# Loads of turned queries moved from SyncE's to ScalarE's DMA queue, and the last projections of a linear-attention and gated-FFN kernel put in a fixed order

## The chip, the cores and the metric

The kernel runs on one core of a Trainium2 chip. The metric is the device time of one launch in microseconds (us), the median of several runs. A core has five engines that run side by side and wait for each other through semaphores: TensorE (PE, matrix products; PEld is its weight load), VectorE (DVE), ScalarE (ACT), GpSimd (POOL) and SyncE (SP), which here only issues DMAs. Each engine executes its own list of instructions strictly in the order of the program: an instruction that waits holds up everything behind it on its engine, DMA issues included.

## The reference

Linear attention with two softmaxes, then a gated feed-forward product. Shapes: q, k, v are 8 batches x 8 heads x 576 positions x 64; x is 4608 tokens x 512; w_a and w_b are 512 x 1536; w_out is 1536 x 512.

```
q_s = exp(q - max(q, -1));  q_s = q_s / (sum(q_s, -1) + 1e-9)     # over the head's 64
k_s = exp(k - max(k, 2));   k_s = k_s / (sum(k_s, 2) + 1e-9)      # over positions
kv  = einsum('bhsd,bhse->bhde', k_s, v)
x   = einsum('bhsd,bhde->bhse', q_s, kv)  -> [B*S, H*D]
out = ((x @ w_a) * (x @ w_b)) @ w_out
```

## The kernel before

The 4608 tokens are cut into 9 chunks (c = 0 to 8) of T = 512. All weights stay on the chip or in scratch memory as pairs of a rounded value and a remainder (`split`, L76: a cast on ACT, a subtraction on DVE), so that each product is three matmuls. While PE works on chunk c, the attention of chunk c + 1 is made in between, in small pieces that the class `Spread` hands out (`attend`).

**The feed-forward part of a chunk.** A loop over i = 0 to 5 (L665) takes two of the twelve 128-wide blocks of w_a and w_b at a time. The products with w_a and w_b are made by a scheme with seven block products instead of eight (`product`, L443, 12 matmuls of 256 columns each, into the PSUM tiles kx, ky, ka, kp), with additions on DVE (u, cc) between them. The weights of each block product, `ws`, come from scratch memory with one DMA of 512 KB each (`get_w`, L165) into eight buffers. The gate's two results per i are split into gh and gl (`g_split`, L437). Their product with w_out (`project`, L463: 4 token blocks t times 3 matmuls of 512 columns, into four PSUM tiles po) is put off: it goes on the list `pend`, and `run_pending` takes it up while the next i is under way. For the last i of the last chunk the two `run_pending` calls in the loop are left out (`if not end`), and all that is pending, the blocks f = 8, 9, 10 and 11, is run after the loop (L724).

**The end of a chunk.** After f = 11 `store` (L473) copies the four po tiles to SBUF (ot) and issues one DMA of 256 KB for each (L481). In chunks 0 to 7 ACT copies the whole row; in the last chunk ACT copies the left half of each row and then DVE the right half.

**The attention of chunks 2 to 8.** The queries are loaded twice. The first load (`q_load`) has tokens on partitions; `q_stats` takes maxima and sums from it, and `q_stats_out` (L330) turns these with a matmul (pst) and writes them to scratch memory (dq, L338). The second load has the queries turned, features on partitions (`q_turned`): per pair of heads g a tile qtt (256 KB, L344) and the maxima and reciprocals of the sums, broadcast over 64 partitions by two DMAs of 256 KB (mr, L347). `q_exp` (L354 on DVE, L355 on ACT) makes the exponentials, splits them into qh and ql, `x_product` (L381) multiplies them with the context into px, and L559 on DVE scales px by the second half of mr into xf. qtt shares two buffers with the keys' tiles (kt), and mr has two buffers: the DMAs for the third g wait until the first g's are done with.

**What sets the order.** Program order is not source order. The kernel is built with `schedule_with_timeline_sim=True`: a scheduler places every instruction on its engine's list by its own estimate of times. `tc.issue_after(ins)` tells it to place what follows not before the instruction named.

Of the kernel before, what the change touches and what calls it, by code (L numbers as in the profile page):

```python
# [23 lines left out]
A11, S2, S3, S1, A12, S4, A22 = range(7)  # L24
B11, T2, T3, T1, B21, B22, T4 = range(7)
# [4 lines left out]
def linear_attention_then_gated_ffn(  # L30
# [18 lines left out]
    nc = tc.nc  # L49
    B, NP, P, J, _, D = k.shape  # L50
# [3 lines left out]
    NF = 2 * NI  # L54
    T = 512
    H = T // 2
    TT = T // P
    NCH = NT // T
    LATE = NCH - qt_late.shape[0]
# [25 lines left out]
    wo = {}  # L85
# [255 lines left out]
    def q_turned(c, g, dq):  # L341

        qt = sb.tile([P, T], F32, name="qtt", tag="kt")
        nc.sync.dma_start(out=qt, in_=qt_late[c - LATE, g])  # L344
        mr = sb.tile([P, 2, T], F32, name="mr", bufs=2)
        for h in range(2):
            nc.sync.dma_start(  # L347
                out=mr[h * D:(h + 1) * D].rearrange("d w t -> d (w t)"),
                in_=dq[g, h].unsqueeze(0).broadcast_to([D, 2 * T]),
            )  # L350
        return qt, mr
# [91 lines left out]
    def product(pt, w, x, first):  # L443

        for n in range(2):
            i = 0
            for c in range(2):
                for wp, xp in ((0, 0), (0, 1), (1, 0)):
                    nc.tensor.matmul(  # L449
                        pt[:, n], w[:, n, wp, c], x[:, xp, c],  # L450
                        start=(first and n == 0 and i == 0), stop=(i == 5),
                        skip_group_check=True,
                    )
                    i += 1

    def project_first(f, g, po):
        for t in range(TT):
            nc.tensor.matmul(
                po[t], g[:, t * P:(t + 1) * P], wo[f][:, 1].bitcast(F32),
                start=(f == 0), stop=(f == NF - 1),  # L460
            )

    def project(f, ghl, po):  # L463
        gh, gl = ghl
        for t in range(TT):
            ts = slice(t * P, (t + 1) * P)
            for i, (a, w) in enumerate(((gh, 0), (gh, 1), (gl, 0))):
                nc.tensor.matmul(  # L468
                    po[t], a[:, ts], wo[f][:, w],
                    start=(f == 0 and i == 0), stop=(f == NF - 1 and i == 2),  # L470
                )

    def store(c, po):  # L473
        for t in range(TT):
            ot = sb.tile([P, DM], F32, name="ot", tag="wr", bufs=4)
            if c == NCH - 1:
                nc.scalar.copy(out=ot[:, 0:H], in_=po[t][:, 0:H])
                nc.vector.tensor_copy(out=ot[:, H:], in_=po[t][:, H:])
            else:
                nc.scalar.copy(out=ot, in_=po[t])  # L480
            nc.sync.dma_start(out=out[c * T + t * P:c * T + (t + 1) * P, :], in_=ot)  # L481
# [168 lines left out]
    def run_pending(last_only=False):  # L650

        if not pend:
            return
        f, ghl, c, po = pend.pop(0)
        (project if c else project_first)(f, ghl, po)
        if f == NF - 1:
            store(c, po)

    last = None
    for c in range(1, NCH):  # L660
        more = c + 1 < NCH
        attend = Spread(attention_tasks(c + 1) if more else [], 3 * NI - 3 - (1 if c == 1 else 0))
        po = None
        x, xo = xo, {}
        for i in range(NI):  # L665
            def operand(op):
                if c > 1:
                    return get_w(i, op)
                if op in (A11, A12, A22):
                    return get_w(i, op)  # L670
                w = split_w(sy[i][op])
                put_w(i, op, w)
                return w

            if more and i == NI - 1:
                x_operands(xfs[c + 1], early, xo)
            kx = ps.tile([P, 2, H], F32, name="kx", tag="k0")
            ky = ps.tile([P, 2, H], F32, name="ky", tag="k1")
            ka = ps.tile([P, 2, H], F32, name="ka", tag="k2")
            cc = sb.tile([P, 4, 2, H], F32, name="cc", bufs=1)  # L680
            u2 = sb.tile([P, 2, H], F32, name="u2", bufs=1)
            u3 = sb.tile([P, 2, H], F32, name="u3", bufs=1)
            if c > 1 or i > 0:
                attend(last)
            if c == 1:
                if i + 1 < NI:
                    sy[i + 1] = sums(i + 1)
                split_wo(2 * i)
                split_wo(2 * i + 1)
            product(kx, operand(A11), x[B11], True)  # L690
            product(ky, operand(S2), x[T2], True)
            nc.scalar.copy(out=u2, in_=kx)
            nc.vector.tensor_tensor(out=u2, in0=ky, in1=u2, op=ALU.add)  # L693
            product(ka, operand(S3), x[T3], True)
            last = nc.vector.tensor_tensor(out=u3, in0=ka, in1=u2, op=ALU.add)
            if more and i == NI - 1:
                x_operands(xfs[c + 1], late, xo)
            end = c == NCH - 1 and i == NI - 1
            if not end:
                run_pending()  # L700
            attend(last)
            kp = ps.tile([P, 2, H], F32, name="kp", tag="k1")
            product(kp, operand(S1), x[T1], True)
            product(kx, operand(A12), x[B21], False)

            nc.vector.tensor_tensor(out=cc[:, 3], in0=kp, in1=u3, op=ALU.add)  # L706
            nc.scalar.copy(out=cc[:, 0, 0], in_=kx[:, 0])  # L707
            nc.vector.tensor_tensor(out=cc[:, 0, 0], in0=kx[:, 1], in1=cc[:, 0, 0], op=ALU.mult)
            last = nc.vector.tensor_tensor(out=cc[:, 3, 0], in0=cc[:, 3, 0], in1=cc[:, 3, 1], op=ALU.mult)
            if not end:  # L710
                run_pending()
            if po is None:
                po = [ps.tile([P, DM], F32, name=f"po{t}") for t in range(TT)]
            attend(last)
            product(kp, operand(S4), x[B22], False)
            nc.vector.tensor_tensor(out=cc[:, 1], in0=kp, in1=u2, op=ALU.add)  # L716
            nc.vector.tensor_tensor(out=cc[:, 1, 0], in0=cc[:, 1, 0], in1=cc[:, 1, 1], op=ALU.mult)  # L717
            g1 = g_split(2 * i, cc[:, 0:2, 0])
            product(ka, operand(A22), x[T4], False)
            nc.vector.tensor_tensor(out=cc[:, 2], in0=ka, in1=u2, op=ALU.add)  # L720
            last = nc.vector.tensor_tensor(out=cc[:, 2, 0], in0=cc[:, 2, 0], in1=cc[:, 2, 1], op=ALU.mult)
            g2 = g_split(2 * i + 1, cc[:, 2:4, 0])
            pend += [(2 * i, g1, c, po), (2 * i + 1, g2, c, po)]
    while pend:  # L724
        run_pending()


# [48 lines left out]
```

## Time and profile before

| | before |
|---|---|
| median of 3 runs (lowest, highest) | 991.0 us (990.97, 994.56) |
| the profiled execution's own time | 986.57 us |
| its span, first to last instruction | 984.5 us |
| DVE, ACT, POOL busy | 632.5, 391.7, 112.8 us |
| mean granted TensorE clock | 0.990 |
| DMA queue q1 (all loads and stores) | 282.57 MB, 81.9% of 16 engines' span |

Busy time is the time in which an engine executes; waiting and the issuing of DMAs are not in it. Idle time before a group of instructions is put down to what ended it. In the rows of the trace an instruction stands as line, engine, operation, tile written <- tiles read, with its number and then busy time and mean duration; SPq is the part of SyncE that waits and issues.

### The profile page before, as it was taken

The numbers are of one execution on the slowest core, as the hardware profiler recorded it, in microseconds if no ns is written. First come the engines' busy times: TensorE is split into PE (matmuls) and PEld (weight loads), VectorE is DVE, ScalarE is ACT, GpSimd is POOL, SyncE is SP. The second block draws the span as 40 slices with busy tenths as digits, with TensorE's granted clock in tenths as the row PEclk, the third lists the DMA queues.
The fourth block names the chain that finished last, engine by engine and source line by source line (L and its number), as shares of the span: only waits on it lengthen the run. The fifth ranks groups of instructions, "written<-read, shape, count | busy, mean of one in ns | idle before, by whom it ended". The sixth has DMA issues, their size and how long they took to land.

```text
span 984.5 us, 16997 instructions
## 1 busy us (share of the span) xinstructions
PE 948.7 (96%) x6171; PEld 854.0 (87%) x6171; DVE 632.5 (64%) x1259; ACT 391.7 (40%) x1087; POOL 112.8 (11%) x96
## 2 busy tenths in 40 slices
PE   3889999999999999999999999999999999999998
PEld 3757666899999999999999999999999999899996
DVE  7797786988686665656566657565656545653443
ACT  8666675542372325322442335223532263221111
POOL 3245344531000000000000000000000000000000
PEclk9799999999999999999999999999999999999999
DMA  9699858999989967997699779977998679767761
GB/s 346 228 412 397 340 207 293 358 332 303 307 279 338 321 241 280 334 334 259 240 339 328 267 258 341 320 264 252 337 295 295 232 282 288 269 230 262 256 212 46
DMA packets 93682, 283.64 MB, mean 288 GB/s; under 512 B 10848, under 2 KB 11424, under 8 KB 93600
## 3 DMA queue, kind: packets, MB, share of 16 engines
q1 hardware_dynamic: 93600, 282.57, 81.9%
q8 instruction: 49, 0.80, 0.3%
q14 instruction: 33, 0.27, 0.1%
HBM read 241.40 MB, written 37.98 MB: 284 GB/s over the span
## 4 chain that ended last, share of the span: by engine, by line
PE 70%; DMA 6%; DVE 2%; ACT 1%; issue 1%; SPq 0%; DVEq 0%
PE po L468 24%; PE kp L449 12%; PE ka L449 12%; PE kx L449 12%; PE ky L449 6%; DMA mr<-dq 4%; DMA qtt<-in_q_late 2%; PE pk L251 2%; PE px L381 2%; DMA dq<-sst 1%; DVE ws L82 0%; ACT qt L323 0%; SPq L347 0%; DVE ql L82 0%; ACT gh L79 0%
## 5 line engine op out<-in xcount | busy, mean ns | idle before, releaser
L468 PE MATMUL po<-wo_w,gh 128*128 128x512 f32 x768 | 226.5, 394 | 1.0 <-ACT gh L79 1.0
L449 PE MATMUL kx<-xo,ws 128*128 128x256 f32 x1152 | 164.8, 284 | 0.0
L449 PE MATMUL ka<-xo,ws 128*128 128x256 f32 x1152 | 163.1, 285 | 0.9 <-DVE cc L720 0.7
L468 PEld LDWEIGHTS po<-wo_w,gh 128*128 128x128 f32 x768 | 138.8, 189 | 27.3 <-ACT gh L79 1.4
L449 PE MATMUL kp<-xo,ws 128*128 128x256 f32 x1152 | 158.3, 284 | 1.1 <-DVE u L693 1.0
L449 PEld LDWEIGHTS ka<-xo,ws 128*128 128x128 f32 x1152 | 152.1, 192 | 4.5 <-DVE cc L720 0.9
L449 PEld LDWEIGHTS kx<-xo,ws 128*128 128x128 f32 x1152 | 151.9, 191 | 3.5 <-issue 0.5
L449 PEld LDWEIGHTS kp<-xo,ws 128*128 128x128 f32 x1152 | 148.2, 191 | 3.9 <-DVE u L693 1.2
L468 PE MATMUL po<-wo_w,gl 128*128 128x512 f32 x384 | 136.9, 395 | 0.0
L79 ACT CAST gh<-cc 128x512 fp32r<-128x512 f32 x96 | 57.6, 620 | 147.4 <-DVE cc L717 144.1
L716 DVE TENSOR_TENSOR cc<-kp,u 128x512 f32<-128x512 f32 x48 | 33.0, 688 | 89.1 <-PE kp L449 88.8
L323 ACT ACTIVATE qt<-qt,st 128x64 f32<-128x64 f32 x224 | 75.0, 336 | 34.7 <-DVE st L320 30.5
L468 PEld LDWEIGHTS po<-wo_w,gl 128*128 128x128 f32 x384 | 71.2, 188 | 15.3
L449 PE MATMUL ky<-xo,ws 128*128 128x256 f32 x576 | 78.5, 285 | 2.5 <-ACT xo L79 2.1
L426 PE MATMUL pt<-xo,ws 128*128 128x512 f32 x288 | 76.1, 415 | 3.0 <-ACT ga L433 3.0
L449 PEld LDWEIGHTS ky<-xo,ws 128*128 128x128 f32 x576 | 72.9, 192 | 3.2 <-ACT xo L79 2.4
L82 DVE TENSOR_TENSOR gl<-cc,gh 128x512 fp32r<-128x512 f32 x96 | 66.9, 704 | 9.6 <-ACT gh L79 9.4
L426 PEld LDWEIGHTS pt<-xo,ws 128*128 128x128 f32 x288 | 55.0, 194 | 19.3 <-ACT ga L433 4.0
L707 ACT COPY cc<-kx 128x256 f32<-128x256 f32 x48 | 17.7, 370 | 130.8 <-PE kx L449 122.1
L706 DVE TENSOR_TENSOR cc<-kp,u 128x512 f32<-128x512 f32 x48 | 32.9, 685 | 54.8 <-PE kp L449 54.8
L219 POOL PARTITION_ALL_REDUCE mx<-m x20 | 14.1, 704 | 467.2 <-DVE m L205 435.4
L355 ACT ACTIVATE qtt<-qtt 128x512 f32<-128x512 f32 x28 | 17.7, 633 | 103.9 <-DVE qtt L354 77.4
(127 smaller groups left out, 1241.8 us busy)
## 6 DMA issues: line engine op xcount, KB each, us to landing
ws<-dw SPq DMA_DIRECT2D x312, 512.0 KB, 5.2
dw<-ws SPq DMA_DIRECT2D x42, 512.0 KB, 5.0
mr<-dq SPq DMA_DIRECT2D x56, 256.0 KB, 6.5
raw<-in_w_ab SPq DMA_DIRECT2D x24, 512.0 KB, 7.9
out<-ot SPq DMA_DIRECT2D x36, 256.0 KB, 4.8
vt<-in_v SPq DMA_DIRECT2D x28, 325.0 KB, 7.3
qt<-in_q SPq DMA_DIRECT2D x32, 256.0 KB, 5.2
kt<-in_k SPq DMA_DIRECT2D x24, 320.0 KB, 5.8
```

Of the source, the lines that this page charges most:

```text
L79: nc.scalar.copy(out=hi, in_=src)
L82: nc.vector.tensor_tensor(out=lo, in0=src, in1=hi.bitcast(F32), op=ALU.subtract)
L251: nc.tensor.matmul(pk, kt[:, j].rearrange("p h d -> p (h d)"), vt[:, j], start=(j == 0), stop=(j == J - 1),)
L323: nc.scalar.activation(out=qt[:, j, h], in_=qt[:, j, h], func=AF.Exp, bias=st[:, h, 0, j:j + 1], accum_out=st[:, h, 1, j:j + 1],)
L355: nc.scalar.activation(out=qt, in_=qt, func=AF.Exp)
L381: nc.tensor.matmul(px[:, s], w, m[:, s], start=(i == 0), stop=(i == 2))
L426: nc.tensor.matmul(pt, w[:, wp], x[g][:, xp], start=(i == 0), stop=(i == 3 * NP - 1))
L449: nc.tensor.matmul(pt[:, n], w[:, n, wp, c], x[:, xp, c], start=(first and n == 0 and i == 0), stop=(i == 5), skip_group_check=True,)
L468: nc.tensor.matmul(po[t], a[:, ts], wo[f][:, w], start=(f == 0 and i == 0), stop=(f == NF - 1 and i == 2),)
L706: nc.vector.tensor_tensor(out=cc[:, 3], in0=kp, in1=u3, op=ALU.add)
L707: nc.scalar.copy(out=cc[:, 0, 0], in_=kx[:, 0])
L716: nc.vector.tensor_tensor(out=cc[:, 1], in0=kp, in1=u2, op=ALU.add)
```

## The change

Three edits. The two loads of `q_turned` are issued by ACT (`nc.scalar.dma_start`), which gives them ACT's DMA queue in place of SyncE's. Everything pending at the end goes behind the last block product (`ka` with A22) and, in f = 10 and 11, the token blocks are kept in turn (three matmuls of one t, then the next t). In the last chunk's `store`, rows are copied whole, t = 0 and 2 by DVE, t = 1 and 3 by ACT.

```diff
     def q_turned(c, g, dq):
 
         qt = sb.tile([P, T], F32, name="qtt", tag="kt")
-        nc.sync.dma_start(out=qt, in_=qt_late[c - LATE, g])
+        nc.scalar.dma_start(out=qt, in_=qt_late[c - LATE, g])
         mr = sb.tile([P, 2, T], F32, name="mr", bufs=2)
         for h in range(2):
-            nc.sync.dma_start(
+            nc.scalar.dma_start(
                 out=mr[h * D:(h + 1) * D].rearrange("d w t -> d (w t)"),
                 in_=dq[g, h].unsqueeze(0).broadcast_to([D, 2 * T]),
             )
...
-    def project(f, ghl, po):
+    def project(f, ghl, po, one_by_one=False):
         gh, gl = ghl
-        for t in range(TT):
-            ts = slice(t * P, (t + 1) * P)
-            for i, (a, w) in enumerate(((gh, 0), (gh, 1), (gl, 0))):
-                nc.tensor.matmul(
-                    po[t], a[:, ts], wo[f][:, w],
-                    start=(f == 0 and i == 0), stop=(f == NF - 1 and i == 2),
-                )
+        with ExitStack() as in_turn:
+            for t in range(TT):
+                ts = slice(t * P, (t + 1) * P)
+                for i, (a, w) in enumerate(((gh, 0), (gh, 1), (gl, 0))):
+                    ins = nc.tensor.matmul(
+                        po[t], a[:, ts], wo[f][:, w],
+                        start=(f == 0 and i == 0), stop=(f == NF - 1 and i == 2),
+                    )
+                if one_by_one:
+                    in_turn.enter_context(tc.issue_after(ins.ins))
 
     def store(c, po):
         for t in range(TT):
             ot = sb.tile([P, DM], F32, name="ot", tag="wr", bufs=4)
-            if c == NCH - 1:
-                nc.scalar.copy(out=ot[:, 0:H], in_=po[t][:, 0:H])
-                nc.vector.tensor_copy(out=ot[:, H:], in_=po[t][:, H:])
+            if c == NCH - 1 and t % 2 == 0:
+                nc.vector.tensor_copy(out=ot, in_=po[t])
             else:
                 nc.scalar.copy(out=ot, in_=po[t])
...
-        (project if c else project_first)(f, ghl, po)
+        if c:
+            project(f, ghl, po, c == NCH - 1 and f >= NF - 2)
+        else:
+            project_first(f, ghl, po)
...
-            product(ka, operand(A22), x[T4], False)
+            last_product = product(ka, operand(A22), x[T4], False)
...
-    while pend:
-        run_pending()
+    with tc.issue_after(last_product.ins):
+        while pend:
+            run_pending()
```

The scheduler moves instructions on all engines but POOL, whose list stays the same, from chunk 1's attention tasks on. Three places matter below.

The first is SyncE's list behind the store of the maxima of chunk 5 (dq_5569), while PE is in chunk 4. Before, the loads of mr and qtt stand between those of the weights (ws):

```order
L338 DMA dq_5569<-sst 64x128
L165 DMA ws<-dw_681 128x1024
L165 DMA ws<-dw_774 128x1024
L347 DMA mr<-dq_5569 64x1024
L344 DMA qtt<-in_q_late 128x512
L347 DMA mr<-dq_5569 64x1024 x3
L165 DMA ws<-dw_2305 128x1024
L165 DMA ws<-dw_2324 128x1024
L165 DMA ws<-dw_2374 128x1024
L195 DMA vt<-in_v 128x650
L344 DMA qtt<-in_q_late 128x512
```

and now SyncE's list goes on with the weights and the values vt alone:

```order
L338 DMA dq_5569<-sst 64x128
L165 DMA ws<-dw_681 128x1024
L165 DMA ws<-dw_774 128x1024
L195 DMA vt<-in_v 128x650
L165 DMA ws<-dw_2305 128x1024
L165 DMA ws<-dw_2324 128x1024
L165 DMA ws<-dw_2374 128x1024
L195 DMA vt<-in_v 128x650
```

All eight mr loads and four qtt loads of the chunk have left the list.

The second place is ACT's list a little later in the same chunk, from the second exponential (L355) to the casts of the gate (gh_5854 and gh_5874 are f = 2 and 3's, which PE's projections read). Before:

```order
L355 ACTIVATE qtt<-qtt 128x512
L79 CAST qh<-qtt 128x512
L79 CAST gh_5854<-cc 128x512
L692 COPY u_5882<-kx 128x512
L79 CAST gh_5874<-cc 128x512
```

and now:

```order
L355 ACTIVATE qtt<-qtt 128x512
L79 CAST qh<-qtt 128x512
L347 DMA mr<-dq_5569 64x1024 x2
L79 CAST gh_5854<-cc 128x512
L344 DMA qtt<-in_q_late 128x512
L79 CAST gh_5874<-cc 128x512
L698 COPY u_5882<-kx 128x512
L347 DMA mr<-dq_5569 64x1024 x2
```

Two loads stand ahead of the first cast and one ahead of the second; the first two wait for L559 to have read the mr tile whose buffer they refill, and the qtt load for DVE's ql.

The third place is the end of PE's list: the last matmuls of f = 9 (gh_10559), the last block product (kp with S4), and the beginning of f = 10 (gh_10663). The four po tiles are 9927 to 9930. Before:

```order
L468 MATMUL po_9927<-wo_w,gh_10559 128x512 x2
L468 MATMUL po_9927<-wo_w,gl_10560 128x512
L468 MATMUL po_9928<-wo_w,gh_10559 128x512 x2
L468 MATMUL po_9928<-wo_w,gl_10560 128x512
L449 MATMUL kp<-xo,ws 128x256 x12
L468 MATMUL po_9929<-wo_w,gh_10559 128x512 x2
L468 MATMUL po_9929<-wo_w,gl_10560 128x512
L468 MATMUL po_9930<-wo_w,gh_10559 128x512 x2
L468 MATMUL po_9930<-wo_w,gl_10560 128x512
L468 MATMUL po_9927<-wo_w,gh_10663 128x512 x2
L468 MATMUL po_9928<-wo_w,gh_10663 128x512 x2
```

and now:

```order
L470 MATMUL po_9927<-wo_w,gh_10559 128x512 x2
L470 MATMUL po_9927<-wo_w,gl_10560 128x512
L449 MATMUL kp<-xo,ws 128x256 x12
L470 MATMUL po_9928<-wo_w,gh_10559 128x512 x2
L470 MATMUL po_9928<-wo_w,gl_10560 128x512
L470 MATMUL po_9929<-wo_w,gh_10559 128x512 x2
L470 MATMUL po_9929<-wo_w,gl_10560 128x512
L470 MATMUL po_9930<-wo_w,gh_10559 128x512 x2
L470 MATMUL po_9930<-wo_w,gl_10560 128x512
L470 MATMUL po_9927<-wo_w,gh_10663 128x512 x2
L470 MATMUL po_9927<-wo_w,gl_10664 128x512
```

Nine matmuls stand between the last block product and f = 10, where there were six. On ACT, the cast of f = 10's gate (gh_10663) now stands ahead of that of f = 11's (gh_10683); before it stood behind it.

More of the change, by code (lines that the diff above doesn't have):

```diff
@@ L454, in product @@
                     i += 1
+        return ins
     def project_first(f, g, po):
@@ L461, in project_first @@
             )
-    def project(f, ghl, po):
+    def project(f, ghl, po, one_by_one=False):
         gh, gl = ghl
-        for t in range(TT):
-            ts = slice(t * P, (t + 1) * P)
-            for i, (a, w) in enumerate(((gh, 0), (gh, 1), (gl, 0))):
-                nc.tensor.matmul(
-                    po[t], a[:, ts], wo[f][:, w],
-                    start=(f == 0 and i == 0), stop=(f == NF - 1 and i == 2),
-                )
+        with ExitStack() as in_turn:
+            for t in range(TT):
+                ts = slice(t * P, (t + 1) * P)
+                for i, (a, w) in enumerate(((gh, 0), (gh, 1), (gl, 0))):
+                    ins = nc.tensor.matmul(
+                        po[t], a[:, ts], wo[f][:, w],
[3 more added lines that the diff above has]
+                    in_turn.enter_context(tc.issue_after(ins.ins))
     def store(c, po):
```

## The prediction

> **What bounds the kernel now.** I read the page's head first, then the busy time by stage, then what PE waited for, and last the chain of waits at the end.
>
> ```profile
> span 984.5 us, 16997 instructions
> PE 948.7 (96%) x6171; PEld 854.0 (87%) x6171; DVE 632.5 (64%) x1259; ACT 391.7 (40%) x1087; POOL 112.8 (11%) x96
> core 0: us, PE busy (x) PEld busy (x) DVE busy (x) ACT busy (x) POOL busy (x), PEclk, DMA share, GB/s
> 0.00:218.00 218.00, 190.16 (x904) 146.39 (x905) 174.30 (x308) 137.91 (x355) 92.35 (x72) 0.95 0.86 324
> 218.00:960.00 742.00, 738.97 (x5155) 690.83 (x5155) 449.02 (x936) 249.95 (x724) 20.44 (x24) 1.00 0.84 286
> 960.00:984.50 24.50, 19.57 (x117) 16.75 (x115) 9.14 (x17) 3.81 (x9) 0.00 (x0) 1.00 0.12 45
> ```
>
> The stages tell more than the 96%. Up to 218 us (loads, chunk 0) PE is idle for 27.8 us, but the change touches nothing there. From 218 to 960 us lies the attention of chunks 2 to 8, whose loads move: PE is busy for 738.97 of 742.00 us, at a full clock. So **all that the moved loads can give back is 3.0 us**, as long as PE does the same work, and its matmuls are the same in number and shape. The last 24.5 us have 4.9 us of idle PE. What PE waited for, from 218 us to the end (us in total, times, longest):
>
> ```profile
> PE px L381 <- DVE ql L82: 1.6, 2, 1.3
> PE kp L449 <- DVE u L693: 1.0, 1, 1.0
> PE po L468 <- ACT gh L79: 1.0, 1, 1.0
> PE px L381 <- ACT qh L79: 0.3, 1, 0.3
> ```
>
> The waits at px (1.6 + 0.3 = **1.9 us**) are what late turned queries cost. The wait at po is the tail's.
>
> **The tail, worked out.** This is the chain from the last block product on (start, length, what):
>
> ```profile
> 970.90 1.44 PE kp L449 x12
> 972.35 0.02 issue
> 972.37 0.70 DVE cc L716
> 973.07 0.02 issue
> 973.10 0.44 DVE cc L717
> 973.53 0.05 ACT gh L79
> 973.58 0.47 issue
> 974.05 0.62 ACT gh L79
> 974.67 0.04 issue
> 974.72 5.86 PE po L468 x24
> 980.57 0.02 issue
> 980.59 0.38 ACT ot L477
> 980.97 0.02 issue
> 981.00 0.42 DVE ot L478
> ```
>
> A projection matmul takes PE 0.232 us here (twelve take 2.78 to 2.80):
>
> ```profile
> 946.77 2.80 PE po L468 x12
> ```
>
> Before, six such matmuls (1.4 us) lie between the end of kp and f = 10, while f = 10's gate needs 2.3 us (972.35 to 974.67), since f = 11's cast stands ahead of its own on ACT (the 0.47 us of "issue"). PE stands still for about 1.0 us, the 1.0 of the waits above. Now nine matmuls (2.1 us) lie there, because kp comes three matmuls earlier, and f = 10's cast comes first: 0.70 + 0.44 + 0.62 and 0.13 of handing over is 1.9 us, within 2.1. The remainder gl follows one DVE subtraction of 0.7 us later, at 2.6 us; PE needs it after two more matmuls, at 2.55. I count at most 0.1 us of wait. **PE ends about 0.95 us earlier.** The first two edits hide the gate behind these nine matmuls; without that cover the wait of 1.0 us would be back.
>
> Then the copies. Before, the last row costs 0.85 us (980.57 to 981.42), as DVE waits for ACT. Now ACT copies it whole; chunks 0 to 7 show the price:
>
> ```profile
> L480 ACT COPY ot<-po 128x512 f32<-128x512 f32 x32 | 18.1, 579 | 2.9 <-PE po L468 1.6 <-PE po L458 0.5
> 979.35 2.43 SPq L481 DMA_DIRECT2D out<-ot  x4
> ```
>
> That is 0.60 us with 0.02 for handing over, 0.25 less. The row before it goes to DVE 0.7 us earlier. No row shows DVE copying a whole row of 512; the half row took 0.42, so it lies between that and twice that, and I take 0.7. It is done before or with the last row, so SyncE is free. The last store lies on the path as before. **Tail: -0.95 - 0.25 = -1.2 us**, between -0.25 (the wait stays) and -1.3.
>
> **The moved loads, worked out.** First what leaves SyncE's list, and how these loads fare (issue time in ns, min/median/max; then size and us to landing, for 218 to 850 us):
>
> ```profile
> L347 SPq DMA_DIRECT2D mr<-dq x56: 450/587/906, 230.8 to 829.9; - x56
> L344 SPq DMA_DIRECT2D qtt<-in_q_late x28: 327/333/535, 239.3 to 825.5; - x28
> ws<-dw SPq DMA_DIRECT2D x251, 512.0 KB, 5.6
> mr<-dq SPq DMA_DIRECT2D x56, 256.0 KB, 6.5
> 829.87 8.96 DMA mr<-dq
> SPq L347 <- DVE xf L559: 29.1, 12, 4.1
> SPq L344 <- DVE ql L82: 17.0, 10, 4.1
> SPq L165 <- PE kp L449: 96.4, 34, 5.6
> ```
>
> SyncE loses 56 x 0.587 + 28 x 0.333 = 42 us of issuing, and the waits of the sixth and seventh row (46 us). I cost that at nothing: SyncE mostly waits for PE to free a weight buffer (96.4 us in the last row alone), and PE never waits for a weight DMA in the list above. What hides it is that SyncE runs up to eight buffers ahead; earlier issue has nothing to bring.
>
> What could bring something is the landing. The mr load that ends in PE's longest wait at px took 8.96 us, though 6.5 is the median and it is half as big as a ws load: it queued behind ws loads. On ACT's queue it need not. The trace of before has no second queue, so I bound it: nothing gained (it lands as late as now) up to the whole 1.9 us of px. To close the longest wait (1.3 us) it would have to land in 7.6 us, still over the median; I take **-1.9**, near that row.
>
> [...]
>
> Against it stands what ACT now does. The issues stand in ACT's list, and their waits stop what is behind them: the casts gh, which PE's projections read, the copies u and cc, and the exponentials. ACT's issuing is not in the trace. At SyncE's prices it is 42 us in all, about 6 a chunk; at least it is nothing. ACT has room on average (250 of 742 us busy); it is lateness that counts. Here is the slack of a cast at the second place of the change (two of ACT's rows, then PE's two projections that read the result):
>
> ```profile
> 526.87 0.62 ACT L79 CAST qh<-qtt 128x512 fp32r<-128x512 f32 x1
> 528.59 0.62 ACT L79 CAST gh<-cc 128x512 fp32r<-128x512 f32 x1 [1.09 <-DVE cc L717]
> 531.39 1.60 PE L449 MATMUL ka<-xo,ws 128*128 128x256 f32 x12
> 532.83 0.63 PE L468 MATMUL po<-wo_w,gh 128*128 128x512 f32 x2
> ```
>
> The cast is done at 529.2 and used at 532.8: 3.6 us. Two mr issues ahead of it cost 2 x 0.587 = 1.2 us and fit. With a wait for xf they may not: SyncE's waits for xf were 29.1 / 12 = 2.4 us on average, which just fits (1.2 + 2.4 = 3.6), and 4.1 at most, which is 1.7 us over. In this place, however, the wait is partly one that ACT has anyway, as the cast qh ahead of the loads already waits for the px matmuls. Over seven chunks I expect one place or so to run over, and allow one wait of the size that PE's list shows for a late DVE or ACT: **+1.0**, between 0 and 7 (one in each chunk).
>
> The scheduler's new order also moves the one wait of kp for u (1.0 us at chunk 1's end); I leave it in, with ends of -1.0 and +1.0.
>
> **The sum.** -1.2 - 1.9 + 1.0 = -2.1 us. The profiled execution took 986.57 us, its span 984.5 with 2.07 around it; it would become 984.5. That execution was 4.4 us quicker than the median of the runs shown, 991.0, so on the median the forecast is **988.9 us**. A measurement of this kernel can tell about 0.5% (5 us) from no change; the forecast is far inside.
>
> **The rivals.**
>
> 1. *The loads land no earlier and cost nothing on ACT*, so that the change does for the middle not what it says. For: PE waits there for only 3.0 us in 742, so nearly everything is hidden already. Against: the 8.96 us landing behind a backlog. Then the tail alone counts: 991.0 - 1.2 = 989.8. Chance 0.30.
>
> 2. *ACT becomes the late engine* (the other side). The mechanism is the mr issue that waits for xf ahead of a gh cast. It decides from the point where the wait and the two issues take over 3.6 us. At the longest wait seen it costs 1.7 us a place, with one place a chunk 7 x 1.7 = 12 us, and with the tail 991.0 + 12 - 1.2 = 1001.8. If only half of the chunks run over it is 995.8. For: SyncE's waits reached 4.1 us, and ACT's list has further loads that wait for dq and for kt's buffers. Against: the px matmuls and the projections have also moved in PE's list, and ACT waited anyway for what these loads wait for. Chance 0.13, a third of it inside 0.5%.
>
> 3. *All of the middle's waits go*, with the tail's: 991.0 - 3.0 - 1.2 = 986.8. For: weights and queries no longer stand in each other's way. Against: a new order has always some wait somewhere; 3.0 us in 742 is already little. Chance 0.12.
>
> The forecast (some of the px waits go, about one new wait comes) has 0.45.
>
> **How the numbers follow.** The cases of rivals 1 and 3 and the forecast lie between 986.8 and about 992 and hold 0.87. For the range I go down to 985.5, since the executions of before differ by up to 4 us, and up to 995.0, which takes in new waits of up to 5 us from rival 2 or from the allowance of 0 to 7. Outside I leave about 0.15. Faster by over 0.5% means under 986.0, which PE's idle time can't give and only a difference between executions could: 0.06. Slower by over 0.5% (above 996.0) is two thirds of rival 2 and a little for disorder that I don't see: 0.10. Within: 0.84.
>
> **What would show it.** For the tail: in the chain at the end no wait of PE ahead of the last 24 matmuls, and one ACT copy of 0.58 us as the last computing step. For the loads: two DMA queues in the page's list, the landing of mr below 6.5 us, and PE's waits for ql and qh at px gone from 218 us on; rival 1 if the median stays at 6.5. For ACT: PE's waits for gh, u or cc in the middle, with a load just ahead of the late instruction on ACT; up to 1 us for the forecast, over 7 for rival 2. The forecast is wrong if PE's idle time in the middle grows by more than a few us, or if the matmuls themselves get slower or faster, which nothing in the change should do.

## The result and the profile after

| | before | after |
|---|---|---|
| median of six runs of each (lowest, highest) | 990.99 us (988.67, 998.46) | 1005.94 us (998.83, 1010.97) |
| ratio of after to before, 95% interval | | 1.0141 [1.0108, 1.0175] |
| the profiled execution's own time | 986.57 us | 1007.73 us |

The changed kernel is 1.4% slower. The forecast of 988.9 us and its range up to 995.0 were both missed, on the slow side. The two profiled executions differ by 21.2 us, and the stages say where. This is the head of the page after and the busy time by stage (the middle is cut at 980 us, where its work ends now):

```profile
span 1005.7 us, 16977 instructions
PE 956.0 (95%) x6171; PEld 858.0 (85%) x6171; DVE 631.1 (63%) x1257; ACT 391.4 (39%) x1085; POOL 113.1 (11%) x96
0.00:218.00 218.00, 189.30 (x899) 144.42 (x900) 171.78 (x307) 137.89 (x355) 92.10 (x72) 0.96 0.85 320
218.00:980.00 762.00, 744.69 (x5141) 694.61 (x5141) 448.42 (x933) 249.10 (x722) 21.03 (x24) 0.99 0.83 279
980.00:1005.70 25.70, 21.99 (x136) 18.99 (x134) 10.89 (x19) 4.41 (x8) 0.00 (x0) 0.97 0.17 62
```

The middle lost everything: PE stands still there for 762.00 - 744.69 = 17.3 us, where it was 3.0, and nearly the same number of matmuls (5141, before 5155) keeps it busy for 5.7 us longer (744.69 against 738.97). What PE waited for from 218 us on, all of it (us in total, times, longest):

```profile
PE px L381 <- ACT qh L79: 7.6, 5, 2.3
PE po L470 <- DVE gl L82: 4.7, 1, 4.7
PE kx L449 <- ACT u L698: 4.3, 1, 4.3
PE ky L449 <- DVE cc L722: 0.4, 1, 0.4
PE px L381 <- DVE ql L82: 0.2, 1, 0.2
```

That is 17.2 us in nine waits, where before it was 3.9 in five. Here is how the moved loads fare now (issue in ns, min/median/max; then size and median us to landing, and landing min/median/max of mr):

```profile
L347 ACTq DMA_DIRECT2D mr<-dq x56: 452/462/1243, 230.6 to 852.1; - x56
L344 ACTq DMA_DIRECT2D qtt<-in_q_late x28: 329/335/588, 239.9 to 846.3; - x28
mr<-dq ACTq DMA_DIRECT2D x56, 256.0 KB, 8.3
DMA to landing us min/median/max: 3.5/8.3/11.2
```

Issuing mr is cheaper than from SyncE (0.462 against 0.587 us), but it lands 1.8 us later than before: 8.3 us, not 6.5.

**The longest standstill, read backwards.** PE stands for 4.73 us until 751.55, for gl. DVE's timeline (start, length, line, what; in brackets the idle time before it and what ended it), with PE's row last:

```profile
742.71 0.68 DVE L726 TENSOR_TENSOR cc<-ka,u 128x512 f32<-128x512 f32 x1
743.43 0.42 DVE L727 TENSOR_TENSOR cc<-cc 128x256 f32<-128x256 f32 x1
750.20 0.69 DVE L354 TENSOR_TENSOR qtt<-qtt,mr 128x512 f32<-128x512 f32 x1 [6.35 <-DMA mr<-dq]
750.81 0.68 DVE L82 TENSOR_TENSOR gl<-cc,gh 128x512 fp32r<-128x512 f32 x1
751.55 0.76 PE L470 MATMUL po<-wo_w,gl 128*128 128x512 f32 x1 [4.73 <-DVE gl L82]
```

The gate's gl needs no load. But it stands behind L354 in DVE's list, L354 waits for mr, and ACT issued that mr at 741.2. DVE is idle for 6.35 us with gl next in line. It was not so before. DVE's list there, before:

```
L720 TENSOR_TENSOR cc<-ka,u_8059 128x512
L82 TENSOR_TENSOR gl_8215<-cc,gh_8214 128x512
L721 TENSOR_TENSOR cc<-cc 128x256
L354 TENSOR_TENSOR qtt<-qtt,mr 128x512
```

and now:

```
L726 TENSOR_TENSOR cc<-ka,u_8059 128x512
L727 TENSOR_TENSOR cc<-cc 128x256
L354 TENSOR_TENSOR qtt<-qtt,mr 128x512
L82 TENSOR_TENSOR gl_8215<-cc,gh_8214 128x512
```

So the scheduler's new order put the addition that waits for the load ahead of gl, and the load then came late.

**The second one** (4.30 us until 856.52, for u). ACT's timeline:

```profile
845.12 1.10 ACTq L347 DMA_DIRECT2D mr<-dq  x2
848.56 3.95 ACTq L347 DMA_DIRECT2D mr<-dq  x2
852.55 0.62 ACT L79 CAST xo<-xf 128x512 fp32r<-128x512 f32 x1 [4.42 <-DMA mr<-dq]
855.36 0.63 ACT L355 ACTIVATE qtt<-qtt 128x512 f32<-128x512 f32 x1 [2.19 <-DVE qtt L354]
855.90 0.57 ACT L698 COPY u<-kx 128x512 f32<-128x512 f32 x1
```

The chain is the same one engine further: u stands behind L355, that behind L354, and that behind the second mr load of 845.12, which landed at 854.6, 9.0 us later. In between ACT itself stood for 3.95 us at two further issues. But ACT was not late with the load that counts. The chain of waits there:

```profile
844.49 0.60 DVE xf L562
845.61 9.01 DMA mr<-dq
854.63 0.70 DVE qtt L354
```

xf, which frees the buffer, ends at 845.09, and ACT issues the pair's first load at 845.12. It is the same in the other three standstills of over 1.9 us: xf ends at 331.54, 439.79 and 740.63, and ACT issues at 331.56, 439.81 and 740.65. What came late there was the landing.

**The clock.** The stretch around the first standstill, cut into windows (start:end, length, busy time of PE, PEld, DVE, ACT, POOL, granted clock, DMA share, GB/s):

```profile
746.80:751.55 4.75, 0.02 (x1) 0.00 (x1) 1.35 (x3) 0.62 (x2) 0.00 (x0) 1.00 0.98 288
751.55:755.10 3.55, 3.55 (x9) 2.79 (x10) 3.55 (x7) 1.62 (x4) 0.00 (x0) 0.52 0.85 291
755.10:758.50 3.40, 3.40 (x26) 3.27 (x25) 1.98 (x3) 1.00 (x2) 0.00 (x0) 1.00 0.42 100
```

After the standstill three projection matmuls take 1.28 us (752.11 to 753.39), where they take 0.70 at full clock: the granted clock is halved for 3.41 us. (The counts of 9 and 26 do not compare, since the 26 are mostly half as wide.) That happens four times in the middle (from 345.4, 451.3, 751.6 and 857.4 us on, each within 1.1 us of the end of a standstill) and costs, as an estimate, half of 3.41 us each, 6.8 in all. Before it happened nowhere in the middle.

**The end** went as predicted. The chain of waits from the last block product on:

```profile
992.50 1.42 PE kp L449 x12
993.93 8.08 PE po L470 x33
1002.00 0.02 issue
1002.03 0.58 ACT ot L483
```

PE runs through 33 matmuls without a gap, and the last row costs one ACT copy of 0.58 us. From the end of kp to the last copy it is 8.7 us (9.1 before), with three matmuls (0.7 us) more in the stretch: 1.1 us gained.

The account of the 21.2 us: 14.3 of standstills in the middle, 6.8 of halved clock, 0.9 of PE's work that fell behind 218 us (189.30 us done by then, before 190.16), less 1.2 of idle PE in the last stage (24.50 - 19.57 = 4.9 before, 25.70 - 21.99 = 3.7 now): 20.8.

### The profile page after: what moved, and what is told of

The parts are those of the page before. It is cut to its first block, busy times and chain, and to the rows that moved or that the text cites. A ratio compares the mean times of both kernels' runs of the same rounds, so it can differ in the third digit from the quotient of the medians.

```text
span 1005.7 us, 16977 instructions
## 1 busy us (share of the span) xinstructions
PE 956.0 (95%) x6171; PEld 858.0 (85%) x6171; DVE 631.1 (63%) x1257; ACT 391.4 (39%) x1085; POOL 113.1 (11%) x96
## 4 chain that ended last, share of the span: by engine, by line
PE 72%; DMA 15%; DVE 7%; ACT 3%; issue 2%; ACTq 0%; DVEq 0%; SPq 0%
PE po L470 22%; PE ka L449 11%; PE kp L449 10%; PE kx L449 10%; DMA mr<-dq 10%; PE ky L449 6%; PE pt L426 5%; DMA qtt<-in_q_late 4%; PE po L459 3%; PE pk L251 3%; PE px L381 2%; DVE ws L82 1%; DVE qtt L354 1%; DMA dq<-sst 1%; DVE wy L104 1%
## 5 line engine op out<-in xcount | busy, mean ns | idle before, releaser
L722 DVE TENSOR_TENSOR cc<-kp,u 128x512 f32<-128x512 f32 x48 | 33.1, 689 | 86.9 <-PE kp L449 86.8
L355 ACT ACTIVATE qtt<-qtt 128x512 f32<-128x512 f32 x28 | 17.7, 632 | 134.2 <-DVE qtt L354 114.3
L354 DVE TENSOR_TENSOR qtt<-qtt,mr 128x512 f32<-128x512 f32 x28 | 19.4, 691 | 77.3 <-DMA mr<-dq 49.1
```

The costliest lines, as they stand in the source:

```text
L354: nc.vector.tensor_tensor(out=qt, in0=qt, in1=mr[:, 0], op=ALU.add)
```

## The experiments

Five theories were tried at first or on the way. **A**: the loads land late on a second queue, and what waits for them holds up PE. **B**: ScalarE is held up by the issues in its list and by what they wait for. **C**: the new order at the end costs. **D**: the two queues wait for each other's transfers. **E**: the fixed order places px and the rest too early for these loads. All ratios are to the kernel before on the same chip, with 95% intervals; "mr" is its median landing.

| run | ratio | mr, us |
|---|---|---|
| tail only, loads on SyncE | 1.0002 [0.9976, 1.0027] | 6.6 |
| both loads on ACT, no tail | 1.0175 [1.0138, 1.0211] | 8.2 |
| both on GpSimd's queue | 1.0029 [1.0004, 1.0055] | 8.0 |
| both on ACT, six weight buffers | 1.0137 [1.0104, 1.0171] | 8.8 |
| qtt alone on ACT | 0.9990 [0.9965, 1.0015] | 7.0 |
| mr alone on ACT | 1.0005 [0.9981, 1.0030] | 7.8 |
| both on ACT, four mr and six weight buffers | 1.0303 [1.0254, 1.0351] | 9.2 |
| copies on ACT, loads on SyncE | 1.0033 [1.0000, 1.0065] | 6.3 |
| copies on ACT, loads on GpSimd | 1.0032 [1.0012, 1.0051] | 7.8 |
| stores on ACT, loads on SyncE | 1.0043 [1.0020, 1.0065] | 6.2 |
| stores on SyncE, loads on SyncE | 0.9976 [0.9959, 0.9993] | 6.5 |
| stores on ACT, loads on GpSimd | 0.9977 [0.9956, 0.9998] | 8.3 |
| both on ACT, px one step later | 1.0106 [1.0062, 1.0149] | 8.0 |
| both on ACT, px two steps later | 1.0130 [1.0080, 1.0181] | 7.0 |
| tail, loads on SyncE, px one step later | 0.9967 [0.9941, 0.9992] | 6.3 |

**Which edit.** The first two runs split the change: the kernel after with its loads back on SyncE's queue, and the kernel before with only this:

```diff
-        nc.sync.dma_start(out=qt, in_=qt_late[c - LATE, g])
+        nc.scalar.dma_start(out=qt, in_=qt_late[c - LATE, g])
...
-            nc.sync.dma_start(
+            nc.scalar.dma_start(
```

> The change without its first edit: mr and qtt are loaded from SyncE's queue again, the order of the last projections and the whole-row copies stay as changed. [...] B (ACT blocked): the loads' own waits stop ACT's list, whatever the landing. C (tail): the new order at the end costs the time. A and B: 1.1 us less than before, ratio 0.999, PE idle from 218 to 960 us about 3 us, no half-clock stretch there. C: ratio about 1.014.

> The first edit alone: mr and qtt from ACT's queue, the end of the kernel as before. A and B: 16 us more than before, ratio 1.013 to 1.018, with mr landing at about 8.3 us and several stretches of half clock. C: ratio 1.000.

The tail gives 1.0002: C falls, and the 1.1 us gained at the end is too small to be measured. The two moved loads alone give 1.0175; they carry the whole loss. In the profiled execution of the tail alone PE was idle for 6.9 us from 218 to 960 us (742.00 - 735.06), not for about 3 as expected. Its longest standstill there was 1.9 us, and the same 6171 matmuls kept PE busy for 1.5 us longer than before (950.2 against 948.7), near the 1.7 us that one stretch of half clock costs, as an estimate: the old queue is not free of standstills. The profiled execution of the loads alone is the quickest of its five (998.75 us, median 1006.68), so its trace shows less than the median loss.

**Late landing alone.** `nc.gpsimd.dma_start` in the same two places takes the issues out of ACT's list and leaves a second queue.

> As e2, but the loads are issued by GpSimd, which has almost nothing to do after 218 us (20 of 742 us busy), so that neither SyncE nor ACT is held up. B: the 16 us go, ratio 0.997 to 1.003, PE waits for px, gh and u of 3 us or less. A: it is a second queue all the same, mr lands at 8 us or later and the ratio is 1.010 to 1.020.

GpSimd's loads land as late as ACT's, and the loss is 0.3%. The page's row of the loads, and PE's waits from 218 us on:

```profile
mr<-dq POOLq DMA_DIRECT2D x56, 256.0 KB, 8.0
PE px L381 <- ACT qh L79: 5.1, 6, 1.6
PE po L468 <- ACT gh L79: 2.4, 2, 1.4
PE px L381 <- DVE ql L82: 0.4, 1, 0.4
```

There are as many waits at px, but none over 1.6 us, and none for gl or u. With this order, then, late landing does not cost 1.4%. The run differs in more than the issuing engine: GpSimd's queue is of another kind on the profile's page (software_dynamic, ACT's is hardware_dynamic), and the scheduler made another order.

**Fewer weights in flight.** Both loads on ACT, and `bufs=8` of ws made 6, so that fewer weights stand in the engines' way.

> As e2, with six buffers for the weights ws in place of eight, so that SyncE has fewer weight loads under way beside ACT's. A: mr's median landing falls from 8.3 to about 7 us and the time by 5 us or more against e2 (ratio to before under 1.010), unless weights now come late (PE would then wait for ws). B: as e2 within 0.3%.

The landing did not fall (8.8 us), and the intervals of the two runs overlap: a miss for A's expectation, since the premise failed.

**Which load.** One of the two on ACT's queue, the other on SyncE's:

> The kernel before with the 28 loads of qtt alone on ScalarE's queue; the 56 of mr stay on SyncE's. A (late landing holds up what reads the loads): qtt lands at about 7.5 us instead of 5.8, mr stays at 6.5, and since DVE's addition L354 waits for both and mr is the later one, little is lost: ratio 1.000 to 1.005. B (ACT's list is held by the issues and their waits): 28 of 84 issues, 28 x 0.335 = 9 us of issuing, waits only for ql: a third or less of the loss, ratio 1.002 to 1.006. The two expect nearly the same here; together with the next run it tells which load carries the 1.7%.

> The kernel before with the 56 loads of mr alone on ScalarE's queue, qtt on SyncE's. A: mr lands at about 8 us, all of the late landing is here: ratio 1.003 (what the loads cost on GpSimd's queue) to 1.017. B: two thirds of the issues, 56 x 0.46 = 26 us of issuing and most of the waits (for L559 to have read the buffer): ratio 1.010 to 1.017.

Neither costs anything that can be measured. B had expected most of the loss with mr alone; that was wrong, and A had expected 1.003 at least. mr alone on ACT lands late too (7.8 us), and costs nothing. The loss does not add up from the two: it appears only where both stand in ACT's list, 84 issues with all that they wait for. Added up from the trace, issuing and the idle time ahead of it, ACT stands at its issues for 45 us with qtt alone, 52 with mr alone, 87 with both (92 in the kernel after).

**More buffers.** Both on ACT, mr with four buffers in the room of two of ws, so that no mr issue waits for L559.

> Both loads on ScalarE's queue as in the run with six weight buffers (ratio 1.0137), but mr has four buffers instead of two, in the room of the two weight buffers. An mr issue then never waits for L559 of the pair two places earlier. A: the landing itself stays at 8 to 9 us, but loads are issued earlier, so that half of the loss or less is left: 1.004 to 1.010. B: the issuing (40 us) stays, the waits ahead of the mr issues go from about 60 us to under 25, ratio 1.003 to 1.007. If the ratio stays at 1.012 or more, neither the waits for the buffer nor the time at which the loads are issued carries the loss, and the issuing or the new order does.

It became twice as bad, against both expectations. The waits of ACT point to a reason (waits for loads' landings, ACT's own list, 218 to 960 us):

```profile
ACT qtt L355 <- DMA mr<-dq: 45.7, 4, 13.0
ACT qtt L355 <- DMA qtt<-in_q_late: 15.7, 1, 15.7
```

These are instructions behind issues that wait for a *landing*, up to 15.7 us. The traces of the kernels before and after show what such issues wait for: the 678 DMAs of SyncE and ACT take eight completion semaphores in turn (84 or 85 landings on each; in the program with GpSimd's loads these have eight others). Of the 670 DMAs that had one before them on their semaphore, none was issued ahead of that one's landing, whichever of the two engines had issued it, and 73 before and 77 after follow it by 0.02 to 0.1 us. Issued earlier, with buffers free, the loads now wait for each other and for weights. The same can be seen on SyncE's side. The longest of its weight loads' waits for landings, before (first row) and after (the other two), 218 to 870 us:

```profile
SPq L165 <- DMA ws<-dw: 3.7, 4, 1.3
```

```profile
SPq L165 <- DMA ws<-dw: 30.9, 14, 4.3
SPq L165 <- DMA mr<-dq: 17.3, 8, 4.8
```

The weight loads that wait 17.3 us in all for mr's landing read nothing of mr. That made theory D.

**Loads in another form.** Three runs meant for B and D changed the transfers themselves: slivers of the loads on ACT (4 of qtt's 128 partitions, 2 of mr's 64, the rest by SyncE), and both mr loads of a pair as one DMA of 512 KB, on ACT, and on SyncE with the new tail:

```diff
-        for h in range(2):
-            nc.sync.dma_start(
-                out=mr[h * D:(h + 1) * D].rearrange("d w t -> d (w t)"),
-                in_=dq[g, h].unsqueeze(0).broadcast_to([D, 2 * T]),
-            )
+        nc.sync.dma_start(
+            out=mr.rearrange("p w t -> p (w t)"),
+            in_=dq[g].unsqueeze(1).broadcast_to([2, D, 2 * T]),
+        )
```

> The kernel before; SyncE still loads nearly all of qtt and mr, but of each load a sliver goes to ScalarE's queue: 4 of qtt's 128 partitions, 2 of each mr load's 64. So ACT's list has the same 84 issues with the same waits, and the bytes stay on SyncE's queue but for 3%. A: mr lands at 6.5 to 7 us as before, PE waits at px for about 2 us in all, ratio 0.998 to 1.004. B: ACT stands as long as in the run with both loads on its queue (about 60 us of waits and 40 us of issuing), PE waits for qh, gh and u of ACT, standstills of 2 us and more are back: ratio 1.008 to 1.017.

> Both loads on ScalarE's queue, but the two mr loads of a pair of heads are one DMA of 512 KB: 56 DMAs in place of 84, the same bytes. D, a new theory: a DMA of SyncE or ScalarE waits until the eighth one before it, of either engine, has landed, so each of the two engines is held by the other's transfers. By D fewer DMAs take fewer of the eight places: the waits of ScalarE's issues for a landing fall from 30 us to 15 or less, those of SyncE's for a landing of ScalarE's queue from 15 us to 7 or less, and the ratio from 1.0175 to 1.007 or less. A (late landing): the bytes are the same, mr as a whole lands no earlier (8 us or later), ratio 1.010 to 1.020. B (ScalarE held, whatever holds it): 28 issues fewer, 13 us, and what D takes away: 1.008 to 1.013.

> A version that might beat both: the changed order and copies at the end, the loads on SyncE's queue, and the two mr loads of a pair as one DMA of 512 KB. 1.1 us from the end, and by D up to 2 us from px's waits: ratio 0.996 to 1.000. If one DMA of 512 KB lands later than two of 256 KB (over 8 us), 1.000 to 1.004.

They took 1.2991 [1.2928, 1.3054], 1.2847 [1.2782, 1.2912] and 1.2430 [1.2378, 1.2482], and their chains of waits say why: one row of the slivers, one of the single DMA on SyncE.

```profile
791.09 21.44 DMA mr<-dq
```

```profile
792.20 27.21 DMA mr<-dq
```

An mr load takes 21 or 27 us to land in these rows, where the median before was 6.5. Why is not shown. The three runs say nothing on B or D, but they show how far late landing alone can go.

**ACT held, without the loads.** Ten copies that nobody reads on ACT behind each L559, with the loads on SyncE and then on GpSimd:

```diff
                 nc.vector.tensor_tensor(out=xfs[c][:, g], in0=px, in1=box["q"][1][:, 1], op=ALU.mult)
+                for _ in range(10):
+                    nc.scalar.copy(out=sb.tile([P, P], F32, name="jk", bufs=1), in_=xfs[c][:, g, 0:P])
```

> The kernel before, all loads on SyncE's queue, and on ScalarE ten copies of 128 x 128 into a tile that nobody reads behind each of the 28 products with mr (L559): 280 x about 0.28 = 80 us of work at the places where the mr loads wait, as much as ScalarE stood at the loads in the run with both on its queue (87 us). No transfer is touched. B: the time held is what counts, ratio 1.010 to 1.018, with standstills of 1.2 us and more at px, gh or u. A and D: the landing stays at 6.5 us and no queue waits for the other: ratio 0.998 to 1.004.

> The run with both loads on GpSimd's queue (1.003) and the one with ten copies on ScalarE behind each L559 (1.003), in one kernel: mr and qtt land late (8 us), and ScalarE is busy for 80 us more at those places, but no issue stands in ScalarE's list and GpSimd's transfers do not take SyncE's turns. A and B together, more than their sum: ratio 1.010 to 1.018. D (the waits for each other's landings are what costs): no more than the sum, 1.002 to 1.008.

The copies took what they should (min/median/max in ns, in the run on SyncE):

```profile
L561 ACT COPY jk<-xf x280: 281/299/305, 252.6 to 865.5; 128x128 f32<-128x128 f32 x140
```

That is 280 x 0.299 = 84 us of ACT, for 0.3%; with late landing besides, still 0.3%. B in its plain form falls, and so does a product of A and B: work that the scheduler knows of is planned around.

**Waits for landings, without the loads.** In place of the copies three stores of 64 KB of xf to scratch memory that nobody reads, issued by ACT, by SyncE, and by ACT with the loads on GpSimd:

```diff
+                jd = dr.tile([3, P, P], F32, name=f"jd{c}_{g}")
+                for j in range(3):
+                    nc.scalar.dma_start(out=jd[j], in_=xfs[c][:, g, j * P:(j + 1) * P])
```

> The kernel before, all loads on SyncE's queue, and on ScalarE's queue three stores of 64 KB of xf (128 x 128) to scratch memory that nobody reads, behind each of the 28 products with mr: 84 issues, with the wait for xf that the mr loads have, and each also waiting for the landing of the eighth transfer before it, as SyncE's loads then wait for these. 5.5 MB more are moved (2%). D: ScalarE stands for 30 us or more at landings, SyncE's waits for landings rise from 20 us to over 60, ratio 1.008 to 1.020. A: mr lands at 6.5 to 7.5 us, ratio 0.999 to 1.005.

> The same 84 stores of xf issued by SyncE: the same eight turns and bytes, but ScalarE's list is free of them; what SyncE waits for (xf, landings) holds up the loads behind it. If D costs time because ScalarE is held: ratio 0.999 to 1.005. If it costs time because SyncE's own loads are held: 1.008 or more, with PE waiting for qh with a late qtt or mr ahead of it.

> Both loads on GpSimd's queue (alone 1.003) and three stores of xf on ScalarE's queue behind each L559 (alone 1.004): late landing, room in PE's order (px behind 18.7, 24.6, 34.3 and 40.4 us of matmuls), and ScalarE held at 84 issues by waits for landings. If late landing and held issues are all that is left with room in the order: ratio 1.006 to 1.013, near the 1.0106 of the run with one empty step. If it takes the loads themselves in ScalarE's list, where a load is issued late because ScalarE is late: 1.002 to 1.006.

84 issues on ACT with their waits for xf and for landings cost 0.4%; on SyncE nothing (the kernel was 0.2% faster); and on ACT together with late landing nothing either, below both ranges expected. In the first of them ACT waited for landings less than D had assumed (18.5 us, not 30 or more), but in the third for 42.5 us, in which it stood at its issues for about 85 us, as long as with both loads on its queue. D alone does not give 1.4%, nor does ACT's standing with late landing, and parts measured one by one do not add up to it. In all these runs the loss came only with both loads themselves in ACT's list.

**Room in the order.** E was read from PE's list. Counted in matmuls (0.232 us for 512 columns) from the transpose of the maxima, the four px of a chunk stand behind 16.0, 20.6, 29.0 and 35.0 us before, 16.5, 21.5, 30.8 and 36.2 after, and 18.6, 24.3, 33.6 and 38.6 with GpSimd's loads. A chunk's chain from its first mr issue to its last xf grew by 4 to 5 us in both (about 35 us before, 39 with both loads on ACT's queue, 40 in the kernel after, 41 with GpSimd's). With GpSimd's queue the order leaves nearly that room; with ACT's queue it leaves 1.2. One or two empty steps in the plan (here with the loads on ACT) move px back:

```diff
-        return seq + pipeline(last)
+        late = pipeline(last)
+        return seq + late[:1] + [[]] + late[1:]
```

> Both loads on ScalarE's queue, and one empty step between a chunk's first load and the rest of its last stage, so that in PE's list the four px stand behind 18.1, 25.2, 33.6 and 39.1 us of matmuls (16.5, 21.5, 30.8, 36.2 without it; 18.6, 24.3, 33.6, 38.6 on GpSimd's queue). Loads and ScalarE's waits stay: mr lands at 8 us or later, ScalarE stands at its issues for about 90 us. E: PE's waits at px and its standstills go, ratio 1.000 to 1.006. A, B and D: 1.012 to 1.020.

> The same with two empty steps: the px behind 24.2, 30.3, 37.6 and 43.4 us. E: as good as with one, 0.998 to 1.006, unless the chunk's end now comes too early for the last px (then PE waits for xo or kx ahead of the next chunk). A, B and D: 1.012 to 1.020.

One step takes 1.0175 to 1.0106, two give 1.0130, with mr landing at 7.0 us. The whole, which E expected, it is not, and even a part is not shown: the intervals overlap (up to 1.0149, from 1.0138), and the kernel after, with the same loads and order in the middle, had 1.0141. A kernel already measured speaks against E as the whole cause too: with mr alone on ACT the first px of the four products, counted in the same way in the trace (medians of six chunks), stand behind 15.8, 22.1, 30.6 and 36.8 us, about as early as with both loads on ACT (16.4, 21.5, 31.5, 36.6), and it loses nothing. What is left in the run with one step looks like the standstill at 751 us. DVE's timeline at its first long one, where PE waited 3.6 us for cc:

```profile
440.50 0.68 DVE L82 TENSOR_TENSOR ql<-qtt,qh 128x512 fp32r<-128x512 f32 x1
446.47 0.69 DVE L354 TENSOR_TENSOR qtt<-qtt,mr 128x512 f32<-128x512 f32 x1 [5.28 <-issue]
447.08 0.68 DVE L717 TENSOR_TENSOR cc<-kp,u 128x512 f32<-128x512 f32 x1
```

L354 again stands ahead of the gate's addition, and it starts as the mr load issued at 435.7 has landed (446.4; the "issue" in the bracket is that landing, which the profile did not put a name to). px has moved, L354 still stands ahead of the gate. That alone is no mark of a slow kernel either: behind the 28 additions L354 the next instruction in DVE's list is one of the gate (cc, u or gl) 7 times before, 12 in the kernel after, 10 with mr alone on ACT and 14 with qtt alone.

**A version meant to beat both.** The tail of the change, the loads on SyncE, and one empty step:

> A version that might beat both: the changed order and copies at the end, the loads on SyncE's queue, and one empty step, px behind 18.0, 24.5, 31.5 and 36.2 us. PE's 1.9 us at px go and the end saves 1.1: ratio 0.995 to 0.999 by E; without a gain at px 0.999 to 1.001.

0.9967 [0.9941, 0.9992]: 986.7 us beside 991.6 for the kernel before in the same runs. PE's waits from 218 us on:

```profile
PE px L381 <- ACT qh L79: 4.1, 4, 1.9
PE kp L449 <- DVE cc L713: 0.2, 1, 0.2
```

The waits at px did not go (4.1 us here, 1.9 before), so the gain is not the one expected; those for u and for the end's gh did. The interval lies wholly under 1, but two kernels with 84 useless stores came out at 0.9976 and 0.9977, so that a gain of this size need not be the step's work.

## Why the prediction was wrong, step by step

- **What bounds the kernel: right.** PE's matmuls did not change, and nothing was won in the middle. But "all that the moved loads can give back is 3.0 us" bounds a gain alone. A list that is full to 99.6% has little to gain and everything to lose.
- **The tail, -1.2 us: right** in mechanism and size (1.1). The nine matmuls cover f = 10's gate, and the last step is an ACT copy of 0.58 us. It is too small to be measured by itself.
- **The landing, -1.9 us, between "it lands as late as now" and 1.9: the step that failed.** It was bounded from one side only; "lands later" was left out, and it lands 1.8 us later (6.5 to 8.3). The sum said that on a queue of its own the load need not queue behind weights, though no row showed a second queue, and the rows showed the engines 84% busy in that stage, whoever issues. It need not, as the traces show now (before, none of the 56 mr loads landed ahead of a transfer issued earlier; after, 14 landed ahead of a weight load that SyncE had issued earlier), but no run shows the 1.9 us: the median landing rose. With this step failed the reading that the waits at px are what late turned queries cost: a late mr now also held gl and u, which read no load, through L354 in DVE's list and L355 in ACT's. The four standstills that brought the half clock each end with an mr that landed 7.8 to 11.2 us after its issue. In place of a gain the middle lost 14.3 us of standstills and 6.8 of halved clock. Late landing alone does not do it (mr alone on ACT lands at 7.8 us, for 1.0005); what makes it costly with both loads is open.
- **ACT's issues, +1.0 us, between 0 and 7: the right sign, by another mechanism and too small.** The issuing itself was priced well (56 x 0.462 + 28 x 0.335 = 35 us, forecast 42). The waits were priced by SyncE's for xf, 2.4 us on average, ahead of a cast gh. PE waited for no gh in the middle, and at the four large standstills ACT issued within 0.04 us of xf. What was not seen is that an issue also waits for landings of the other engine's transfers: ACT's issue of 852.06 came 0.02 us after the load of 845.12 had landed.
- **"The scheduler's new order also moves the one wait of kp for u; ends of -1.0 and +1.0": the order was read at ACT's and PE's lists, not at DVE's.** The place of the longest standstill, L354 ahead of gl, stood in DVE's list of the changed kernel and could be read.
- **The clock was not in the sum.** Four standstills of 1.93 us and more brought about 6.8 us on top of their own 13.3.
- **The rivals.** Rival 2, ACT as the late engine, had the side and most of the size (1001.8 at one place a chunk, 1005.9 measured), but the casts gh were the wrong place: PE waited for qh, gl and u. That the size comes near is luck. Its chance of 0.13 rested on ACT's waiting anyway for what these loads wait for. Rival 1 had the loads do no harm, the forecast 1 us of it.

**What is shown, and what stays open.** Shown: the loss comes with the two loads together in ACT's list; landing is later on both second queues that were tried (medians of 8.3 and 8.0 us, 6.5 before); in the kernel after, the two longest standstills are gate instructions behind L354 or L355 in the in-order lists of DVE and ACT, which waited for a load that landed 9 us after its issue. Not shown is why both loads together cost 1.4 to 1.75% where each alone costs nothing, and how that is shared between later landings, ACT's waits at its issues and the places that the scheduler gave px, L354 and L355. GpSimd's run has another order as well as another queue, since the scheduler makes its order from the issuing engine; the same order with another queue was not tried.

## What to carry to other kernels

Moving the loads to another engine's queue moved three things here: which transfers they land behind (14 of 56 mr loads passed a weight load, before none), which instruction list their waits hold up, and the scheduler's order of everything that reads them; bound each from both sides, with "later" as one end. In a kernel whose busiest engine is idle for 0.4% of a stage, read the new order on every engine for one pattern: an instruction that waits for a load, newly ahead of one that the busiest engine needs. Such places cost nothing while the load lands in time, so ask of each how late it may land. In this kernel an engine with nothing urgent in its list was the better place for loads that leave SyncE's (GpSimd 1.003, ScalarE 1.0175).

## What the runs showed of the hardware

- **A second queue delivered later, not sooner.** mr took 6.5 us from SyncE, 8.3 from ACT, 8.0 from GpSimd, with the 16 engines 83 to 84% busy in that stage; landings of 8.9 and 9.0 us ended the two longest standstills. Over all runs with whole mr loads it was 6.2 to 7.0 from SyncE, 7.0 to 9.2 from ACT and 7.8 to 8.3 from GpSimd. Why is not shown.
- **The clock halved after short standstills, but not after each.** Standstills of 1.93 to 4.73 us were followed by 3.41 us of half clock in the kernel after (one of 1.86 was not). In the run with GpSimd's queue, where PE's longest wait was 1.6 us, a matmul of 218 to 960 us kept PE busy for 0.1443 us on average (734.58 us for 5090), between 0.1434 before (738.97 for 5155) and 0.1449 after (744.69 for 5141, to 980 us); from this, as an estimate, shorter standstills were enough there. With mr alone on ACT, with a wait of 2.7 us, it was 0.1435, as before. With qtt alone one of 2.4 us was not followed by half clock, as the windows around it show (the clock is the third figure from the end):

```profile
343.30:345.80 2.50, 0.10 (x2) 0.03 (x1) 1.94 (x4) 1.25 (x2) 0.00 (x0) 1.00 1.02 402
345.80:349.20 3.40, 3.40 (x28) 3.40 (x29) 2.84 (x6) 1.62 (x3) 0.00 (x0) 1.00 0.98 375
```

  In the clock record of the trace of the kernel after the four stretches of half clock begin at 345.43, 451.25, 751.62 and 857.43 us and last 3.413 us each; the full clock between them lasts 102.40, 296.96 and 102.40 us, which is 30, 87 and 30 times that length. Why a standstill of 1.93 us was followed by half clock and one of 2.4 us was not is not shown.
